# Where an attention + MLP-mixer kernel computes the flag that decides on its general path

## The chip, the cores and the metric

The kernel runs on one core of one Trainium2 chip. The metric is the device time of one execution in microseconds (us), as the median over runs. The engines are TensorE (PE, whose weight loads are shown apart as PEld), VectorE (DVE), ScalarE (ACT), GpSimd (POOL) and SyncE (SP). Each has its own instruction stream and runs it in order; an instruction can wait for semaphores that other engines or landed DMAs count up.

## The reference, cut to what matters

Batch 8, 8 heads, 576 positions, head size 64. For each batch and head the kernel computes causal attention with a bias that comes from a running sum of `s`, and over the result (576 x 512 per batch) an MLP mixer: two products over positions, then two over channels.

```
cum    = cumsum(max(s, 0))
scores = q @ k.T / 8  + min(-(cum[i] - cum[j]), 0)      (j <= i)
x      = softmax(scores) @ v, heads side by side          (576 x 512)
u      = x + (relu(x.T @ w_tok1) @ w_tok2).T
out    = u + relu(u @ w_ch1) @ w_ch2
```

The fast path of the kernel drops far-away blocks of the attention and takes no maximum before the exponential. That is only right for inputs whose bias falls fast enough and whose q and k are small. So the kernel also computes, on the chip, one number that says whether any row breaks these conditions, reads it into a register on every engine, and branches: at zero the kernel ends, above zero a second, slow and general path (`general`) computes everything again. With these inputs the number is zero, and the branch jumps over the code of the general path.

## The kernel before

A small planner in the kernel (`Plan`) takes a list of operations with their dependencies, the engines that can run them, and an estimated cost, simulates the engines, and emits the instructions in the order of the starting times that come out. On PE the operation with the lowest `prio` among those that can start first is taken; a PE operation's `prio` is a pair whose first number is a rank, some 4 per batch.

For each batch `b` the operations are made in this order: loads, transposes and scores of q and k (`quad`, `pair`), the attention products, the token products (`tok`), and the channel products (`chan`). `chan` has two halves:

- L1106: for each of 12 blocks of 128 hidden channels, four matmuls write a tile `pmx` in PSUM, and ACT or DVE (L1113, L1115) evacuate it with a relu into `gb` (odd batches) or `ga`. The last batch is odd and has 320 columns twice, so 24 such tiles.
- L1131: for each of the five chunks of 128 positions, 12 matmuls write a `pmx` tile, DVE adds `u` (L1139) into a tile `of`, and SP stores it (L1144, L1147). In the last batch the fifth chunk is done in two halves of 256 columns.

There are four `pmx` tiles (128 x 512, one PSUM bank each), taken in turn.

The flag is made of four steps at the end of the list. DVE writes the tile `bad` (64 x 4 gaps and 128 x 32 sums of squares against their bounds, L1210). PE sums `bad` over the partitions with a matmul against a column of ones (L1214), into one row of 36 values of a `pmx` tile. DVE sums that row (L1219) and casts it to an integer (L1220), `flagi`. Behind the planned part, `nc.values_load(flagi)` (L1255) makes every engine load the value into a register (TENSOR_LOAD), and `tc.If` (L1258) makes every engine compare and branch. The code behind the branch (rows of L1258 and L1285 in the profile) sets semaphores to what they would be behind the general path, and SP waits there for every semaphore of the kernel before all engines meet and the program ends.

The matmul of the flag has `prio=(100, 0)`: its rank is above that of all others (the last batch's channel products have ranks up to 42), so PE does it last. The two DVE steps have `prio=50`.

Of the kernel before, what the change touches and what calls it, by code (L numbers as in the profile page):

```python
# [246 lines left out]
def c_pe(n, f32=False):  # L247
    occ = n * (4 if f32 else 1) / 2400.0 + 0.0025
    return occ, occ + 0.21
# [131 lines left out]
def kernel(  # L381
# [14 lines left out]
    B, H, S, D = q.shape  # L396
# [21 lines left out]
    def sb(name, shape, dt, pool=None):  # L418
        return (pool or const).tile(shape, dt, name=name, tag=name)
# [44 lines left out]
    P = Plan()  # L464
# [52 lines left out]
    for i in range(2, 4):  # L517
        P.op({"DVE": (0.3, 0.5, lambda i=i: pads(nc.vector, i)), "POOL": (0.4, 0.6, lambda i=i: pads(nc.gpsimd, i))},
             writes=[("pad", i)], prio=40)
    P.op({"DVE": (0.6, 0.8, lambda: pads2(nc.vector)), "POOL": (1.0, 1.2, lambda: pads2(nc.gpsimd))},  # L520
         writes=["padw"], prio=41)
    P.op({"DVE": (0.3, 0.5, lambda: pads3(nc.vector, 1)), "POOL": (0.5, 0.7, lambda: pads3(nc.gpsimd, 1))},
         writes=["padv"], prio=42)
# [12 lines left out]
    def dve(n, fn, two=False):  # L536
        return {"DVE": (*c_dve(n, two), fn)}
# [7 lines left out]
    for ti, src in enumerate((k, q)):  # L545
# [4 lines left out]
        for f in range(2):  # L550
            def cast0(eng, ti=ti, f=f):
# [4 lines left out]
                else:  # L556
# [3 lines left out]
                 reads=[("stage", ti)], writes=[(first, ti, f)], prio=-6)  # L560
    P.op({"SP": (0.6, 4.8, lambda: nc.sync.dma_start(out=s_sb[:, :], in_=s.rearrange("b h s -> (b h) s")))},
         writes=["s"], prio=-7)
    P.op(dve(576, lambda: nc.vector.tensor_scalar_max(out=s_sb[:, :], in0=s_sb[:, :], scalar1=0.0)),
         reads=["s"], writes=["sr"], prio=-1)
    scan = P.op({"DVE": (1.3, 1.6, lambda: nc.vector.tensor_tensor_scan(
        out=cum[:, :], data0=one_sb[:, :], data1=s_sb[:, :], initial=0.0, op0=ALU.mult, op1=ALU.add))},
        reads=["sr"], writes=["cum"], prio=2)
    P.op(dve(1, lambda: nc.vector.tensor_scalar(
        out=half[:, :], in0=cum[:, S - 1 : S], scalar1=-0.5, scalar2=None, op0=ALU.mult)),
        reads=["cum"], writes=["half"], prio=-1)  # L570
    P.op(act(576, lambda: nc.scalar.activation(
        out=wn[:, 0:S], in_=cum[:, :], func=AF.Exp, bias=half[:, 0:1], scale=1.0), True),
        reads=["half", "cum"], writes=["wn"], prio=-5)
    P.op({"ACT": (1.0, 1.1, lambda: nc.scalar.copy(out=neg[:, :, :],
                                                   in_=zero[:, :].unsqueeze(1).to_broadcast([128, 2, 512])))},
         writes=["neg0"], prio=-6)
# [33 lines left out]
    bad = sb("bad", [128, 4 + NSQ], FP32, fast)  # L610
# [346 lines left out]
    def either(n, fa, fd, two=False):  # L957
        return {"ACT": (*c_act(n), fa), "DVE": (*c_dve(n, two), fd)}
# [131 lines left out]
    def chan(b, u, us, uT):  # L1090
        P.shift = SHIFT["chan"][b]
        odd = b % 2
        rank = 4 * (b + 1) + LAG
        g = Buf(r_gb if odd else r_ga)
        spans = [(0, 256), (256, 640)] if b == 1 else [(0, 320), (320, 640)] if odd else [(0, 256), (256, 512)] if b == 0 else [(0, 512)]
        for (cc, (a, e)) in ([(cc, sp) for hf in range(2) for sp in spans for cc in range(6 * hf, 6 * hf + 6)] if b < 2 else
                             [(cc, sp) for cc in range(NCC) for sp in spans]):
            if True:
                ukeys = ([(uT, c, m) for c in range(2) for m in range(NMC)] if b < 1 and a == 0 else
                         [(uT, c) for c in range(a // 128, (e + 127) // 128)])  # L1100
                pm = Buf(r_mx, False)
                n = e - a

                def mm(cc=cc, pm=pm, a=a, e=e):
                    for m in range(NMC):
                        nc.tensor.matmul(out=pm.t[:, 0 : e - a], lhsT=wc1[:, m, cc * 128 : cc * 128 + 128],  # L1106
                                         rhs=uT.t[:, m, a:e], start=(m == 0), stop=(m == NMC - 1))
                P.op({"PE": (4 * c_pe(n)[0], 4 * c_pe(n)[0] + 0.21, mm)},
                     reads=ukeys + [("wc1", cc // (NCC // 2) * 2 + m) for m in range(2)],
                     writes=[(pm, 0)],  # L1110
                     holds=[g], prio=(rank + (cc // 6 + 0.05 * (cc % 6) + 0.4 * (a > 0) if b < 2 else 2.0 * cc / NCC), 0)).late = 2.0
                P.op(either(n,
                            lambda cc=cc, pm=pm, a=a, e=e: nc.scalar.activation(  # L1113
                                out=g.t[:, cc, a:e], in_=pm.t[:, 0 : e - a], func=AF.Relu),
                            lambda cc=cc, pm=pm, a=a, e=e: nc.vector.tensor_scalar_max(  # L1115
                                out=g.t[:, cc, a:e], in0=pm.t[:, 0 : e - a], scalar1=0.0)),
                     reads=[(pm, 0)], writes=[(g, cc, a)], prio=0)
        for ci, c in enumerate((4, 0, 1, 2, 3) if odd else (0, 1, 2, 3)):
            if odd:
                src, si = (us, 0) if c == NJ - 1 else (u, c)  # L1120
            else:
                src, si = u, c
            sk = [(us, 0, 0), (us, 0, 64)] if src is us else [(u, si, 0)]
            o = Buf(r_o, False)
            whole = b < B - 1 or ci < NJ - 1
            for (na, ne) in ([(0, DM)] if whole else [(0, DM // 2), (DM // 2, DM)]):
                pm = Buf(r_mx, False)
                for th in range(3):
                    def mm(c=c, pm=pm, th=th, na=na, ne=ne):
                        for cc in range(th * 4, th * 4 + 4):  # L1130
                            nc.tensor.matmul(out=pm.t[:, na:ne], lhsT=g.t[:, cc, c * 128 : c * 128 + 128],  # L1131
                                             rhs=wc2[:, cc, na:ne], start=(cc == 0), stop=(cc == NCC - 1))
                    occ = 4 * c_pe(ne - na)[0]
                    P.op({"PE": (occ, occ + 0.21, mm)},
                         reads=[(g, cc, a) for cc in range(th * 4, th * 4 + 4) for (a, e) in spans] + [("wc2", i) for i in range(th * 4 // 3, (th * 4 + 3) // 3 + 1)],
                         writes=[(pm, 0)], holds=[o], prio=(rank + 2.0 + 2.0 * ci / NJ, 1 + (na > 0)))

                def add(pm=pm, o=o, src=src, si=si, na=na, ne=ne):
                    nc.vector.tensor_tensor(out=o.t[:, na:ne], in0=pm.t[:, na:ne], in1=src.t[:, si, na:ne], op=ALU.add)  # L1139
                P.op(dve(ne - na, add), reads=[(pm, 0)] + sk, writes=[(o, na)], prio=0)  # L1140

                def st(o=o, c=c, na=na, ne=ne):
                    if c < NJ - 1:
                        nc.sync.dma_start(out=out[b, c * 128 : c * 128 + 128, na:ne], in_=o.t[:, na:ne])  # L1144
                    else:
                        for i in range(2):
                            nc.sync.dma_start(out=out[b - 1 + i, NQ:S, :], in_=o.t[i * 64 : i * 64 + 64, :])  # L1147
                P.op({"SP": (0.6 if c < NJ - 1 else 1.2, 0, st)}, reads=[(o, na)], prio=0, dma=128 * 0.088 / 16)
# [36 lines left out]
    for b in range(B):  # L1185
        for h in range(0, H, 4):
            quad(b, h)
        st = tok(b)
        chan(b, *st)
        P.shift = 0.0  # L1190
        if b == 2:
            behind(b, st[2])
            stage_in(5)
            stage_in(6)
        if b == 3:
            behind(b, st[2])
            stage_in(7)
        if b == B - 3:
            behind(b, st[2])
            for i in range(2):  # L1200
                for h in range(0, H, 4):
                    stage_sq(i, h)
# [3 lines left out]
        reads=["wn", "late"], writes=["pre"], prio=50)  # L1206
# [5 lines left out]
        reads=[("sq", i) for i in range(NSQ)] + ["bad0"], writes=["bad"], prio=50)  # L1212
    bf = Buf(r_mx, False)
    P.op({"PE": (0.3, 0.6, lambda: nc.tensor.matmul(out=bf.t[0:1, 0 : 4 + NSQ], lhsT=ones[:, :], rhs=bad[:, :],  # L1214
                                                    start=True, stop=True))},
         reads=["bad"], writes=[(bf, 0)], prio=(100, 0))

    def flag():
        nc.vector.tensor_reduce(out=flagf[:, :], in_=bf.t[0:1, 0 : 4 + NSQ], op=ALU.add, axis=mybir.AxisListType.X)  # L1219
        nc.vector.tensor_copy(out=flagi[:, :], in_=flagf[:, :])  # L1220
    P.op({"DVE": (0.4, 0.7, flag)}, reads=[(bf, 0)], writes=["flag"], prio=50)

    order = P.run()
    rest = [1.2]
# [65 lines left out]
```

## Time and profile before

| what | us |
|---|---|
| median of 3 runs | 297.11 (296.98 to 297.3) |
| the profiled execution, its own time | 297.6 |
| its span, first to last instruction | 295.8 |
| PE busy | 284.9 |
| granted TensorE clock, mean | 0.997 |

The profiled execution took 297.6 us, of which 295.8 us are its span; 1.8 us lie around it. The profile's own views are: the page (busy time of each engine, groups of instructions), the chain of waits (followed back from the last piece of engine work), the instructions of one line, the waits of one engine, the timeline, and the DMA queues. Times in a row are microseconds from the span's start unless they are marked ns. A `q` behind an engine's name (DVEq, SPq) marks what its sequencer does by itself: waits, register loads, branches, DMA issues.

### The profile page before, as it was taken

To read this page: it belongs to the slowest core of one execution; us is meant where nothing else is said; L and a number is where in the kernel's file an instruction comes from. 1 tells how busy PE (TensorE), PEld (TensorE's weight loads), DVE (VectorE), ACT (ScalarE), POOL (GpSimd) and SP (SyncE) were. 2 spreads that over 40 slices of the span, in tenths; PEclk is the share of its full clock that TensorE was granted. 3 is DMA by queue.
4 is the path that set the end of the run, shared out by engine and by line. 5 is a ranking of instruction groups with operands and counts; after the bars stand their busy time and mean duration, and the time that the engine had idled before them with its cause. 6 is when DMAs were issued, how large, how long until landed. Compare 5 with 4: busy or idle time off the path is not lost.

```text
span 295.8 us, 7107 instructions
## 1 busy us (share of the span) xinstructions
PE 284.9 (96%) x2852; PEld 167.8 (57%) x2885; DVE 196.3 (66%) x425; ACT 195.3 (66%) x311; POOL 82.8 (28%) x147
## 2 busy tenths in 40 slices
PE   8999999999999999999999999999999999999991
PEld 3468665676745555546754555457765544457550
DVE  5894669999999969997577658767679524110030
ACT  5786877889999488996865467047999344227300
POOL 8645669688001954019000000017000000000000
PEclk9999999999999999999999999999999999999998
DMA  7999999999906899759915200259904311320032
GB/s 222 225 207 208 204 211 234 200 248 204 193 9 137 167 261 236 120 133 170 219 25 123 74 35 2 57 142 160 196 4 74 107 71 38 89 106 2 7 106 75
DMA packets 38344, 39.22 MB, mean 133 GB/s; under 512 B 17600, under 2 KB 30976, under 8 KB 38304
## 3 DMA queue, kind: packets, MB, share of 16 engines
q0 software_dynamic: 17072, 24.25, 44.7%
q1 hardware_dynamic: 21232, 14.44, 17.8%
q8 instruction: 24, 0.39, 0.5%
q14 instruction: 16, 0.13, 0.2%
HBM read 40.65 MB, written 9.44 MB: 169 GB/s over the span
## 4 chain that ended last, share of the span: by engine, by line
PE 74%; DMA 14%; DVE 4%; POOL 3%; issue 2%; POOLq 0%; DVEq 0%
PE pmx L1131 28%; PE pmx L1106 28%; DMA vf<-in_v_dram 8%; DMA wc<-in_moe_w_ch_dram 6%; PE pmx L987 4%; PE pmx L1049 4%; PE psc L886 4%; PE psc L803 4%; PE pmx L746 2%; POOL vf L644 1%; DVE ub L1056 1%; POOL qkn L491 1%; DVE vp L662 1%; DVE x L919 1%; DVE h L1001 0%
## 5 line engine op out<-in xcount | busy, mean ns | idle before, releaser
L823 ACT ACTIVATE E<-psc 128x1024 bf16<-128x1024 f32 x64 | 62.1, 1022 | 27.1 <-PE psc L803 27.0
L1106 PEld LDWEIGHTS <-wc 128*128 128x128 bf16 x624 | 58.9, 98 | 32.1 <-issue 0.5
L1106 PE MATMUL pmx<-uTb,wc 128*128 128x320 bf16 (+2 forms) x384 | 55.7, 299 | 0.5 <-DVE gb L1115 0.5
L1131 PE MATMUL pmx<-wc,gb 128*128 128x512 bf16 (+1 forms) x243 | 54.0, 369 | 0.7 <-issue 0.3
L1106 PE MATMUL pmx<-uTa,wc 128*128 128x512 bf16 (+1 forms) x234 | 45.3, 336 | 0.3
L1113 ACT ACTIVATE gb<-pmx 128x320 bf16<-128x320 f32 (+2 forms) x65 | 28.3, 438 | 24.7 <-PE pmx L1106 20.0
L1131 PE MATMUL pmx<-wc,ga 128*128 128x512 bf16 x186 | 43.6, 379 | 0.5 <-issue 0.2
L1131 PEld LDWEIGHTS <-gb 128*128 128x128 bf16 x252 | 23.9, 98 | 24.5
L678 ACT ACTIVATE junk<-qkn 128x1152 bf16<-128x1152 bf16 x32 | 37.3, 1166 | 0.5
L1113 ACT ACTIVATE ga<-pmx 128x512 bf16<-128x512 f32 (+1 forms) x45 | 24.1, 545 | 19.2 <-PE pmx L1106 18.5
L644 POOL DMA_DIRECT2D vf<-in_v_dram x39 | 33.4, 870 | 3.8 <-DMA vf<-in_v_dram 1.9
L1131 PEld LDWEIGHTS <-ga 128*128 128x128 bf16 x192 | 17.9, 98 | 20.1
L662 DVE TENSOR_TENSOR vp<-vf,wT 128x512 bf16<-128x512 f32 (+1 forms) x39 | 26.0, 712 | 1.1 <-DMA vf<-in_v_dram 0.8
L886 PEld LDWEIGHTS <-E 128*128 128x128 bf16 x576 | 21.2, 97 | 5.0
L919 DVE TENSOR_TENSOR x<-psc,rc 128x640 bf16<-128x640 f32 x28 | 23.0, 820 | 0.7
L832 DVE TENSOR_TENSOR E<-E,keep 128x512 bf16<-128x512 bf16 x56 | 22.4, 414 | 1.3 <-ACT E L823 1.2
L471 POOL CAST seen<-uTb 1x1 f32<-1x1 bf16 x10 | 2.0, 198 | 74.6 <-DMA uTb<-ub 70.5
L1139 DVE TENSOR_TENSOR of<-pmx,ua 128x512 f32<-128x512 f32 x16 | 11.3, 707 | 15.5 <-PE pmx L1131 9.7
L769 DVE COPY kT<-pmx 128x576 bf16<-128x576 bf16 x20 | 14.6, 751 | 9.6 <-PE pmx L746 9.5
L803 PEld LDWEIGHTS <-kT 64*128 64x128 bf16 x320 | 12.9, 94 | 13.8 <-issue 11.8
L886 PE MATMUL psc<-vp,E 128*128 128x65 bf16 x522 | 20.5, 193 | 0.0
L769 DVE COPY qT<-pmx 128x576 bf16<-128x576 bf16 x21 | 15.2, 752 | 8.0 <-PE pmx L746 7.3
(119 smaller groups left out, 336.7 us busy)
## 6 DMA issues: line engine op xcount, KB each, us to landing
vf<-in_v_dram POOLq DMA_DIRECT2D x32, 256.0 KB, 7.8
out_dram<-of SPq DMA_DIRECT2D x31, 256.0 KB, 2.1
qkn<-in_k_dram POOLq DMA_DIRECT2D x19, 288.0 KB, 7.2
qkn<-in_q_dram POOLq DMA_DIRECT2D x19, 288.0 KB, 7.8
wc<-in_moe_w_ch_dram POOLq DMA_DIRECT2D x8, 384.0 KB, 8.5
out_dram<-of SPq DMA_DIRECT2D x10, 128.0 KB, 2.3
vf<-in_v_dram POOLq DMA_DIRECT2D x7, 128.0 KB, 8.3
gb<-in_k_dram SPq DMA_DIRECT2D x1, 576.0 KB, 3.8
```

What stands on the lines that cost most here:

```text
L644: nc.gpsimd.dma_start(out=vf.t[p0 : p0 + n, c, :, :], in_=v[b, :, c * 128 : c * 128 + n, :].rearrange("h p d -> p h d"))
L662: eng.tensor_tensor(out=vp.t[p0 : p0 + n, c, :, 0:D], in0=vf.t[p0 : p0 + n, c, :, :], in1=wT[p0 : p0 + n, cw, b * H : b * H + H].unsqueeze ...
L678: nc.scalar.activation(out=junk[:, :].rearrange("p (t n) -> p t n", t=2), in_=i, func=AF.Square, accum_out=sq[:, col : col + 1])
L769: nc.vector.tensor_copy(out=o, in_=i)
L803: nc.tensor.matmul(out=ps.t[:, hh * 512 + c0 : hh * 512 + c0 + e - a], lhsT=kT.t[hh * 64 : hh * 64 + 64, j0 : j0 + 128], rhs=qT.t[hh * 64 ...
L823: nc.scalar.activation(out=E.t[:, :, 512 * pc : 512 * pc + 512], in_=ps.t[:, :].rearrange("p (e n) -> p e n", e=2), func=AF.Exp, scale=0.125)
L832: nc.vector.tensor_tensor(out=o, in0=o, in1=keep[:, :].unsqueeze(1).unsqueeze(1).to_broadcast([128, 2, 2, 128]), op=ALU.mult)
L886: nc.tensor.matmul(out=o[:, ic, 0:DE], lhsT=E.t[:, hh, d0 : d0 + 128], rhs=vp.t[:, jc, h + 2 * hh, 0:DE], start=(jc == j_lo), stop=(jc == ic))
L919: nc.vector.tensor_tensor(out=x.t[:, :, :].rearrange("p c (g f e d) -> p g e f c d", f=2, e=2, d=D)[:, h // 4, h % 2], in0=pav2()[:, :, :, ...
L1106: nc.tensor.matmul(out=pm.t[:, 0 : e - a], lhsT=wc1[:, m, cc * 128 : cc * 128 + 128], rhs=uT.t[:, m, a:e], start=(m == 0), stop=(m == NMC ...
L1113: lambda cc=cc, pm=pm, a=a, e=e: nc.scalar.activation(out=g.t[:, cc, a:e], in_=pm.t[:, 0 : e - a], func=AF.Relu),
L1131: nc.tensor.matmul(out=pm.t[:, na:ne], lhsT=g.t[:, cc, c * 128 : c * 128 + 128], rhs=wc2[:, cc, na:ne], start=(cc == 0), stop=(cc == NCC - 1))
```

## The change

`chan` of the last batch notes the PE operation that makes the last of the 24 tiles of L1106 under the name "last". The flag's matmul now also depends on it and has rank 0 instead of 100: the planner puts it as soon as this product is done, ahead of the products of L1131. The two DVE steps have `prio` 0 instead of 50. Nothing else is edited, and what is computed is the same. Line numbers behind the two new lines are higher by 2: the flag's matmul is L1216, the DVE steps are L1221 and L1222, the adds L1141, the stores L1146 and L1149, the register loads L1257, the branch L1260.

```diff
@@ chan, behind the loop over the 24 tiles
+        if b == B - 1:
+            P.writer["last"] = P.ops[-2]
         for ci, c in enumerate((4, 0, 1, 2, 3) if odd else (0, 1, 2, 3)):
...
     P.op({"PE": (0.3, 0.6, lambda: nc.tensor.matmul(out=bf.t[0:1, 0 : 4 + NSQ], lhsT=ones[:, :], rhs=bad[:, :],
                                                     start=True, stop=True))},
-         reads=["bad"], writes=[(bf, 0)], prio=(100, 0))
+         reads=["bad", "last"], writes=[(bf, 0)], prio=(0, 0))
...
-    P.op({"DVE": (0.4, 0.7, flag)}, reads=[(bf, 0)], writes=["flag"], prio=50)
+    P.op({"DVE": (0.4, 0.7, flag)}, reads=[(bf, 0)], writes=["flag"], prio=0)
```

What the build makes of it, at three places. In the rows, `of_112` to `of_115` are the four output tiles, `pmx_118` to `pmx_121` the four PSUM tiles, `gb_111` the evacuated hidden channels, `wc_70` and `wc_71` the channel weights, and the names in brackets are the counters that an instruction waits for (DVE_49, PE_49, Activation_49 of the engines, DMAHW of landed stores).

DVE at the end of the program, before:

```order
L1139 TENSOR_TENSOR of_115<-pmx_121,us_107 128x512 [waits DVE_49,DMAHW5_49,PE_49,Activation_49]
L1139 TENSOR_TENSOR of_112<-pmx_120,ub_105 128x512 [waits DVE_49,DMAHW6_49,PE_49,Activation_49]
L1139 TENSOR_TENSOR of_113<-pmx_118,ub_105 128x512 [waits DVE_49,DMAHW7_49,PE_49,Activation_49]
L1139 TENSOR_TENSOR of_114<-pmx_119,ub_105 128x512 [waits DVE_49,DMAHW0_49,PE_49,Activation_49]
L1139 TENSOR_TENSOR of_115<-pmx_121,ub_105 128x256 [waits DMAHW1_49,DMAHW2_49,DVE_49,PE_49]
L1139 TENSOR_TENSOR of_115<-pmx_120,ub_105 128x256 [waits PE_49]
L1219 TENSOR_REDUCE flagf<-pmx_118 1x1 [waits PE_49]
L1220 CAST flagi<-flagf 1x1 [waits DVE_49]
L1255 TENSOR_LOAD flagi [waits DVE_49]
L1258 COMPARE_AND_BRANCH
```

DVE at the same place now:

```order
L1221 TENSOR_REDUCE flagf<-pmx_121 1x1 [waits PE_49]
L1222 CAST flagi<-flagf 1x1 [waits DVE_49]
L1141 TENSOR_TENSOR of_115<-pmx_120,us_107 128x512 [waits DMAHW5_49,PE_49,Activation_49]
L1141 TENSOR_TENSOR of_112<-pmx_118,ub_105 128x512 [waits DMAHW6_49,PE_49,Activation_49]
L1141 TENSOR_TENSOR of_113<-pmx_119,ub_105 128x512 [waits DMAHW7_49,PE_49,Activation_49]
L1141 TENSOR_TENSOR of_114<-pmx_121,ub_105 128x512 [waits DMAHW0_49,PE_49]
L1141 TENSOR_TENSOR of_115<-pmx_120,ub_105 128x256 [waits DMAHW1_49,DMAHW2_49,DVE_49,PE_49]
L1141 TENSOR_TENSOR of_115<-pmx_118,ub_105 128x256 [waits PE_49]
L1257 TENSOR_LOAD flagi [waits DVE_49]
L1260 COMPARE_AND_BRANCH
```

The two steps of the flag stand ahead of the last batch's six adds, and the register load follows directly on the last add. Four of the adds have one wait less, each of them an instruction of its own: DVE's code ahead of the branch is four instructions shorter.

SP ahead of the branch, before:

```order
L1144 DMA out_dram<-of_114 128x512 [waits DMAHW0_49,DVE_49]
L1147 DMA out_dram<-of_115 64x512 [waits DMAHW1_49,DVE_49]
L1147 DMA out_dram<-of_115 64x512 [waits DMAHW2_49]
L1144 DMA out_dram<-of_112 128x512 [waits DMAHW3_49,DVE_49]
L1144 DMA out_dram<-of_113 128x512 [waits DMAHW4_49,DVE_49]
L1144 DMA out_dram<-of_114 128x512 [waits DMAHW5_49,DVE_49]
L1144 DMA out_dram<-of_115 128x256 [waits DMAHW6_49,DVE_49]
L1144 DMA out_dram<-of_115 128x256 [waits DMAHW7_49,DVE_49]
L1255 TENSOR_LOAD flagi [waits DVE_49]
L1255 ISA x2
L1258 COMPARE_AND_BRANCH
```

SP at the same place now:

```order
L1146 DMA out_dram<-of_114 128x512 [waits DMAHW0_49,DVE_49]
L1257 TENSOR_LOAD flagi [waits DVE_49]
L1257 ISA x2
L1149 DMA out_dram<-of_115 64x512 [waits DMAHW1_49,DVE_49]
L1149 DMA out_dram<-of_115 64x512 [waits DMAHW2_49]
L1146 DMA out_dram<-of_112 128x512 [waits DMAHW3_49,DVE_49]
L1146 DMA out_dram<-of_113 128x512 [waits DMAHW4_49,DVE_49]
L1146 DMA out_dram<-of_114 128x512 [waits DMAHW5_49,DVE_49]
L1146 DMA out_dram<-of_115 128x256 [waits DMAHW6_49,DVE_49]
L1146 DMA out_dram<-of_115 128x256 [waits DMAHW7_49,DVE_49]
L1260 COMPARE_AND_BRANCH
```

SP's load of the flag, and its wait for it, have moved ahead of the last batch's seven stores; its branch stays behind them.

PE between the last tile of L1106 and the first chunk of L1133 (L1131 before) now:

```order
L1106 LDWEIGHTS wc_70
L1106 MATMUL pmx_119<-uTb_109,wc_70 128x320
L1216 MATMUL pmx_121<-bad,ones 1x36 [waits Activation_49]
L1133 LDWEIGHTS gb_111
L1133 MATMUL pmx_120<-wc_71,gb_111 128x512 [waits Activation_49]
```

Before, the matmul of the flag was PE's last one, behind the last product of the two half chunks. Now the flag takes the `pmx` tile that the first chunk had, and the chunks move on by one tile. On ACT and POOL nothing moves: their load of the flag follows their last work (evacuations, loads of q and k) as before, and on PE it follows its last product.

## The prediction

> **What bounds the kernel now.** I read the page first, then the chain of waits from 270 us on, then the lines of the register load and the branch, since the change can only act there.
>
> ```profile
> span 295.8 us, 7107 instructions
> ...
> PE 284.9 (96%) x2852; PEld 167.8 (57%) x2885; DVE 196.3 (66%) x425; ACT 195.3 (66%) x311; POOL 82.8 (28%) x147
> ```
>
> PE is busy for 96% of the span, and the change takes no product from it. What is left is the tail. The chain's last rows (start, us, what):
>
> ```profile
> 289.30 0.42 DVE of L1139
> 289.72 0.10 DVE flagf L1219
> 289.82 0.02 issue
> 289.85 0.14 DVE flagi L1220
> ```
>
> The last add runs from 289.30 to 289.72, the flag's two steps end at 289.85 + 0.14 = 289.99, and engine work is over. The span goes on for another 5.8 us. The lines of the load and the branch show what is in them (each row: count, then ns of one as min/median/max, then first and last start):
>
> ```profile
> L1255 ACTq TENSOR_LOAD <-flagi x1: 467/467/467, 290.0 to 290.0; - x1
> L1255 POOLq TENSOR_LOAD <-flagi x1: 492/492/492, 290.0 to 290.0; - x1
> L1255 DVEq TENSOR_LOAD <-flagi x1: 546/546/546, 290.0 to 290.0; - x1
> L1255 PEldq TENSOR_LOAD <-flagi x1: 492/492/492, 290.0 to 290.0; - x1
> L1255 SPq TENSOR_LOAD <-flagi x1: 538/538/538, 290.1 to 290.1; - x1
> ```
>
> ```profile
> L1258 SPq EVENT_SEMAPHORE  x8: 17/17/17, 291.6 to 292.1; - x8
> L1258 ACTq COMPARE_BRANCH  x1: 50/50/50, 290.5 to 290.5; - x1
> L1258 POOLq COMPARE_BRANCH  x1: 45/45/45, 290.6 to 290.6; - x1
> L1258 PEldq COMPARE_BRANCH  x1: 3773/3773/3773, 290.6 to 290.6; - x1
> L1258 DVEq COMPARE_BRANCH  x1: 72/72/72, 290.6 to 290.6; - x1
> L1258 SPq COMPARE_BRANCH  x1: 58/58/58, 291.1 to 291.1; - x1
> L1258 POOLq EVENT_SEMAPHORE  x1: 17/17/17, 291.1 to 291.1; - x1
> L1258 ACTq EVENT_SEMAPHORE  x1: 17/17/17, 293.6 to 293.6; - x1
> L1258 PEldq EVENT_SEMAPHORE  x1: 51/51/51, 294.5 to 294.5; - x1
> L1258 DVEq EVENT_SEMAPHORE  x1: 21/21/21, 294.7 to 294.7; - x1
> ```
>
> All five engines wait for the flag, load it in about 0.5 us and branch. COMPARE_BRANCH is the jump, and EVENT_SEMAPHORE the first instruction behind it: POOL and SP are back after 0.5 us, ACT after 3.1, PE after 3.9, DVE only after 4.1. SP then waits for all others (waits of SP, then its rows of the closing line):
>
> ```profile
> SPq L1285 <- DVEq L1258: 2.0, 1, 2.0
> ```
>
> ```profile
> L1285 SPq EVENT_SEMAPHORE  x14: 17/28/2038, 292.2 to 295.8; - x14
> ```
>
> SP's longest wait, 2.0 us, is ended by DVE's first instruction behind the jump at 294.7; 1.1 us later the span ends. So the chain that sets the end is: last add, flag, DVE's load at 290.0, DVE's jump (back at 294.7), closing steps to 295.8. From the start of DVE's load to the end: 5.8 us.
>
> What fills the jump are fetches of code: in 290 to 296 us (a DMA view; one slice of the GB/s row is 0.15 us)
>
> ```profile
> GB/s 0 0 0 41 280 341 205 7 0 0 164 0 55 55 55 0 0 0 0 0 0 0 0 0 0 0 0 0 55 0 0 0 0 0 109 55 0 0 0 0
> ...
> q8 instruction: 2, 0.03, 2.4%
> q14 instruction: 6, 0.05, 2.4%
> ```
>
> the bytes up to 291.2 are the last store, those from 291.5 (slice 10) on are instructions, 0.9 us behind the branches at 290.6. [...]
>
> **The change part by part.** *The flag's inputs.* They are ready long before:
>
> ```profile
> L1210 DVE TENSOR_SCALAR bad<-sq x1: 170/170/170, 230.9 to 230.9; 128x32 f32<-128x32 f32 x1
> ```
>
> ```profile
> L1113 ACT ACTIVATE gb<-pmx x24: 437/437/437, 263.8 to 276.3; 128x320 bf16<-128x320 f32 x24
> ```
>
> `bad` is there at 231 us. The `pmx` tile that the flag takes is the oldest of the last four, evacuated four steps before ACT's last one at 276.3, so PE does not wait for it. The flag is then due at about 277, while DVE idles: its reduce and cast (0.17 + 0.14 us) cost nothing there.
>
> *SP's load.* It now waits for the flag ahead of the seven stores. SP's next store (timeline):
>
> ```profile
> 278.97 0.69 DVE L1139 TENSOR_TENSOR of<-pmx,us 128x512 f32<-128x512 f32 x1 [15.00 <-PE pmx L1131]
> 279.68 1.12 SPq L1147 DMA_DIRECT2D out_dram<-of  x2
> ```
>
> is at 279.68; a load from 277 to 278 is over by then. Nothing, with some 1.7 us to spare.
>
> *ACT and POOL* jump at about 278 and are back long before the end: off the path.
>
> *PE.* The matmul of the flag leaves the end and enters the stream of products. Its rows at the old place (timeline):
>
> ```profile
> 289.19 0.09 PEld L1214 LDWEIGHTS pmx<-bad,ones 128*1 128x1 f32 x2 [0.21 <-issue]
> 289.19 0.23 PE L1214 MATMUL pmx<-bad,ones 128*1 128x36 f32 x2
> ```
>
> Two passes of 194 ns end 0.23 us after the first began, so the second starts 0.04 us behind the first: at least 2 x 0.04 = 0.08 us. At most it is idle time and both passes, 0.21 + 0.23 = 0.44. The idle time holds the streaming of the product ahead of it, which a stream of products has anyway, so I take 0.2, nearer the lower end. All of L1131, the last add and the last store come 0.2 us later: last add at 289.50.
>
> *DVE's load* no longer waits for the flag, but stands right behind the last add. Does it start while that add still runs, or behind it? No row shows a load there. The nearest one is DVE's wait instructions behind adds:
>
> ```profile
> 263.28 0.69 DVE L1139 TENSOR_TENSOR of<-pmx,ua 128x512 f32<-128x512 f32 x1 [1.90 <-DMA out_dram<-of]
> ...
> L1139 DVEq EVENT_SEMAPHORE  x3: 21/2436/15559, 263.4 to 279.1; - x3
> ```
>
> The first starts at 263.4 while its add runs until 263.97, the last at 279.1 beside the add of 278.97: the sequencer goes on within 0.1 us. I take the same for the load: 289.50 + 0.05 = 289.55. The other bound is the add's end, 289.50 + 0.42 = 289.92.
>
> *The sum.* DVE's load starts at 289.55 instead of 290.0; everything behind it, 5.8 us, is taken as it is, DVE's 4.1 us stall included, since its own row is the nearest. End at 295.35 instead of 295.8: 0.45 us less. What would be late next: PE's load can start at 289.0 + 0.2 = 289.2 and it is back 4.5 us later, at 293.7, DVE at 289.55 + 4.7 = 294.25. SP branches behind the last store:
>
> ```profile
> L1144 SPq DMA_DIRECT2D out_dram<-of x1: 332/332/332, 289.8 to 289.8; - x1
> ```
>
> at 289.8 + 0.2 + 0.33 = 290.3, and came to its wait for DVE 1.6 us behind its branch (291.1 to 292.7), so at about 292.0. DVE stays last. The profiled execution would take 297.6 - 0.45 = 297.15; it lies 0.5 above the median of the runs, so on the median 297.11 - 0.45 = 296.66.
>
> A measurement of this kernel can tell about 0.2%, 0.6 us, from no change. The forecast lies just inside it. With the flag's matmul at its bounds (0.08 to 0.44) it is 296.5 to 296.9.
>
> **The rivals.** *The stalls shrink.* Before, three far jumps fetch at once, ACT's first (3.1 us), then PE's (3.9) and DVE's (4.1). Now ACT's is 11 us earlier and PE's 0.3 or more ahead of DVE's. If waiting for each other made the last ones long, DVE needs 3.1 us: back at 289.55 + 0.6 + 3.1 = 293.25, and PE's return at 293.7 and the closing 1.1 us end the span at 294.8, 1.0 less: 296.1; with PE at 3.1 too, DVE is last again and the end is 294.35: 295.65. The order of the three speaks for it; that packets are done well before any return (the last of the first bunch at 292.25, DVE back at 294.7) speaks against. A second way to this end: DVE's code is four instructions shorter, so its target may now lie in code that is resident, as POOL's and SP's do; then PE's 293.7 is last: 296.1. [...]
>
> *DVE's load is held until the last add has ended.* Then it starts at 289.92 + 0.05 = 289.97, and 0.05 us are left: 297.05. The wait instructions above speak against it, but they touch no data, and a load reads memory. [...]
>
> *Slower: DVE's fetch meets the last store.* Before, the store's bytes were through at 291.2 and instructions came from 291.5. Now the store is 0.2 later and the fetch, 0.9 us behind a branch at 290.15, is due at 291.05, inside it. The store lands
>
> ```profile
> DMA to landing us min/median/max: 1.7/1.7/1.7
> ```
>
> 1.7 us after its issue at 290.0, at 291.7. If the fetch is only served then, DVE is back 0.65 later than in the sum: 0.2 slower than before, 297.3. It decides once the fetch waits longer than 0.45 us. Against it: the store's bytes use few of the slices, and only 128 KB are left.
>
> **How the numbers follow.** Forecast as summed 0.40, shrinking stalls 0.34, held load 0.16, the store in the way 0.07, something not seen 0.03. The likeliest gives 296.65. The range goes from the lower rival's end, 295.6, to 297.2, beyond the held load; left out is the slower case and what was not seen. Faster by over 0.2% (below 296.5): the shrinking stalls and the lower edge of the forecast, 0.40. Slower by over 0.2% (above 297.7) needs more than the store's 0.2 us: 0.04. Within: 0.56.
>
> **What would show it.** Right: the flag's cast at about 277, SP's load over before 279.9, ACT and POOL back before 283; the last add at 289.5; DVE's load starting within 0.1 us of it, and DVE back 4.7 us later, still the last one that SP waits for; span 295.3. The shrinking stalls show as DVE back in under 3.6 us after its branch, the held load as a load behind 289.9, the store as instruction packets later than 1.2 us behind DVE's branch. The prediction is wrong if the stream of products is stretched by more than 0.44 us, or if SP waits last for another engine than DVE or PE.

## The result, and the profile after

| | us |
|---|---|
| before, median of 6 runs | 297.11 (296.71 to 297.3) |
| after, median of 6 runs | 294.91 (294.62 to 295.22) |
| ratio | 0.9928, 95% interval 0.9915 to 0.9941 |
| profiled execution after, its own time | 294.74 |
| its span | 292.9 |

The kernel is 2.2 us faster (1.8 to 2.5 by the interval). The forecast was 0.45. The two spans differ by more, 2.9 us, because the part ahead of the tail also lies at another place in each execution: a second profile of the kernel before, below, has its last add 1.0 us later than the first with the same code. So the tail is compared from the start of the last add.

First the end of the chain of waits after (start, us, what):

```profile
269.90 5.57 PE pmx L1106 x41
275.47 0.15 PE pmx L1216 x2
275.63 13.10 PE pmx L1133 x72
...
288.75 0.42 DVE of L1141
```

The flag's matmul (L1216) is a link of PE's stream now, and the last engine work is the last add. From its start at 288.75 to the end of the span it is 4.1 us; before it was 295.8 - 289.30 = 6.5. The tail is 2.4 us shorter. The timeline around the flag shows what was paid for that:

```profile
274.63 0.84 PE L1106 MATMUL pmx<-uTb,wc 128*128 128x320 bf16 x5
...
275.40 0.23 PE L1216 MATMUL pmx<-bad,ones 128*1 128x36 f32 x2
...
275.56 4.92 PE L1133 MATMUL pmx<-wc,gb 128*128 128x512 bf16 x22
275.67 0.18 DVE L1221 TENSOR_REDUCE flagf<-pmx 1x1 f32<-1x36 f32 x1 [12.50 <-PE pmx L1216]
275.88 0.14 DVE L1222 CAST flagi<-flagf 1x1 int32<-1x1 f32 x1
...
279.14 1.13 SPq L1149 DMA_DIRECT2D out_dram<-of  x2
```

The products of L1106 follow each other by 0.136 us (5.57 / 41 in the chain), so behind the five from 274.63 on the next one could have started at 274.63 + 5 x 0.136 = 275.31. It starts at 275.56: the flag costs the stream 0.25 us. That and the shorter tail make -2.4 + 0.25 = -2.15 us, about the 2.2 between the medians.

The register loads and the branch (count, ns of one as min/median/max, first and last start):

```profile
L1257 SPq TENSOR_LOAD <-flagi x1: 479/479/479, 276.1 to 276.1; - x1
...
L1257 PEldq TENSOR_LOAD <-flagi x1: 487/487/487, 286.6 to 286.6; - x1
L1257 DVEq TENSOR_LOAD <-flagi x1: 546/546/546, 288.8 to 288.8; - x1
```

```profile
L1260 SPq EVENT_SEMAPHORE  x8: 17/17/17, 290.1 to 291.2; - x8
L1260 ACTq COMPARE_BRANCH  x1: 50/50/50, 276.6 to 276.6; - x1
...
L1260 POOLq EVENT_SEMAPHORE  x1: 17/17/17, 277.1 to 277.1; - x1
L1260 ACTq EVENT_SEMAPHORE  x1: 17/17/17, 279.3 to 279.3; - x1
L1260 PEldq COMPARE_BRANCH  x1: 3877/3877/3877, 287.2 to 287.2; - x1
L1260 DVEq COMPARE_BRANCH  x1: 72/72/72, 289.4 to 289.4; - x1
...
L1260 DVEq EVENT_SEMAPHORE  x1: 21/21/21, 290.0 to 290.0; - x1
L1260 PEldq EVENT_SEMAPHORE  x1: 51/51/51, 291.1 to 291.1; - x1
```

The reader is to see three things. ACT and POOL are done at 279. DVE loads beside its last add, at 288.8, as forecast, but it is back 0.6 us behind its branch, not 4.1. And PE loads at 286.6 and jumps at 287.2, while its products run on until 288.7; its 3.9 us jump is over at 291.1, where the forecast had 293.7.

So who is last? SP's longest waits from 288 us on, its closing rows, the last store's landing, and the queues of code in 288 to 294 us:

```profile
SPq L1260 <- SPq L1260: 1.1, 3, 0.5
SPq L1287 <- PEq L1287: 0.7, 2, 0.5
```

```profile
L1287 SPq EVENT_SEMAPHORE  x14: 17/28/28, 291.2 to 292.8; - x14
```

```profile
DMA to landing us min/median/max: 1.9/1.9/1.9
```

```profile
q8 instruction: 2, 0.03, 2.2%
q14 instruction: 3, 0.02, 1.4%
```

No wait of SP names an engine's jump any more (PEq L1287 is the meeting of the engines), and none of its closing waits is longer than 0.028 us, where one took 2.038 before. What SP is held by now is the landing of the last store: issued at 289.2 and 1.9 us under way, it is down at 291.1; the eighth of SP's rows on L1260, its wait for this store, follows at 291.2, and the closing waits and the meeting take the last 1.7 us. PE is back at 291.1 too, but SP's closing waits come to PE's counter only at 291.8, 0.7 us later. Three packets of code come on q14 in these six us, where there were six: two at 290.6 and 290.7, and one at 293.5, behind the end of the span. None lies between DVE's branch (289.4) and its return (290.0). The bound has passed from a jump to the stores.

### The profile page after: what moved, and what is told of

Read it like the earlier page. It is cut to its first block, busy times and chain, and to the rows that moved or that the text cites. A ratio compares the mean times of both kernels' runs of the same rounds, so it can differ in the third digit from the quotient of the medians.

```text
span 292.9 us, 7136 instructions
## 1 busy us (share of the span) xinstructions
PE 286.8 (98%) x2885; PEld 167.5 (57%) x2885; DVE 196.5 (67%) x425; ACT 195.0 (67%) x311; POOL 82.8 (28%) x147
## 4 chain that ended last, share of the span: by engine, by line
PE 76%; DMA 13%; DVE 5%; POOL 3%; issue 1%; POOLq 0%; DVEq 0%
PE pmx L1133 29%; PE pmx L1106 28%; DMA vf<-in_v_dram 7%; DMA wc<-in_moe_w_ch_dram 6%; PE pmx L987 5%; PE pmx L1049 4%; PE psc L886 4%; PE psc L803 4%; PE pmx L746 2%; DVE vp L662 1%; POOL qkn L491 1%; DVE x L919 1%; DVE ub L1056 1%; POOL seen L471 1%; POOL vf L644 1%
## 5 line engine op out<-in xcount | busy, mean ns | idle before, releaser
L1106 PEld LDWEIGHTS <-wc 128*128 128x128 bf16 x624 | 58.9, 98 | 31.8 <-issue 0.2
L1106 PE MATMUL pmx<-uTb,wc 128*128 128x320 bf16 (+2 forms) x384 | 55.7, 300 | 0.2 <-DVE gb L1115 0.2
L1133 PE MATMUL pmx<-wc,gb 128*128 128x512 bf16 (+1 forms) x252 | 55.0, 369 | 0.0
L1106 PE MATMUL pmx<-uTa,wc 128*128 128x512 bf16 (+1 forms) x240 | 45.6, 337 | 0.0
L1133 PE MATMUL pmx<-wc,ga 128*128 128x512 bf16 x192 | 44.5, 380 | 0.0
L1133 PEld LDWEIGHTS <-gb 128*128 128x128 bf16 x252 | 23.7, 98 | 24.5
L1133 PEld LDWEIGHTS <-ga 128*128 128x128 bf16 x192 | 17.9, 98 | 20.1
L1141 DVE TENSOR_TENSOR of<-pmx,ua 128x512 f32<-128x512 f32 x16 | 11.3, 709 | 15.0 <-PE pmx L1133 9.3
L803 PE MATMUL psc<-qT,kT 64*128 64x256 bf16 (+2 forms) x320 | 20.3, 250 | 0.0
```

What stands on the lines that cost most here:

```text
L803: nc.tensor.matmul(out=ps.t[:, hh * 512 + c0 : hh * 512 + c0 + e - a], lhsT=kT.t[hh * 64 : hh * 64 + 64, j0 : j0 + 128], rhs=qT.t[hh * 64 ...
```

## The experiments

Two reasons why DVE's 4.1 us are gone were to be told apart: its code ahead of the branch is four instructions shorter, so that its target may have come near; and three far jumps no longer start at once. The rival was that the flag's place alone explains the gain. Below, a jump is called near where the engine is back in 0.6 us or less, and far where it needs 2.4 us or more; "resident" is the author's word for code at which an engine is back before any packet of code has come, as POOL before (back at 291.1, first packet at 291.5). Where the code lies is in no profile. Each ratio is to the kernel before, timed on the same chip.

**DVE's target moved back.** Four steps that are never executed are put into the general path on DVE:

```diff
+            gz = gp.tile([128, 8], FP32, name="gz", tag="gz")
+            for i in range(4):
+                nc.vector.memset(gz[:, i : i + 1], 0.0)
```

> The changed kernel with four small DVE memsets added inside the general path, which is not executed: no instruction that runs is different, but the code that DVE jumps over is four instructions longer, so its target stands where it stood before the change. Theory A (the target had come into code that was resident): DVE's return from the jump takes 4.1 us again instead of 0.6, DVE is last again, back at about 293.5 in the changed kernel's times, and the time is 294.91 + 1.7 = 296.6, close to the recorded forecast; if a fetch without ACT's beside it takes 3.1 us, 295.6. Theory B (DVE's return was short because no other engine was fetching): nothing changes, 294.9.

Measured: 295.92 us (10 runs), ratio 0.9961 (0.9946 to 0.9975). Branch rows and SP's wait (lines are 3 higher):

```profile
L1263 DVEq COMPARE_BRANCH  x1: 72/72/72, 289.6 to 289.6; - x1
...
L1263 PEldq EVENT_SEMAPHORE  x1: 51/51/51, 291.3 to 291.3; - x1
L1263 DVEq EVENT_SEMAPHORE  x1: 21/21/21, 292.6 to 292.6; - x1
```

```profile
SPq L1290 <- DVEq L1263: 0.7, 1, 0.7
```

The far jump is back, and with it the wait of SP for DVE, but at 3.0 us and not at 4.1; the page counts one packet of code more on q14 than that of the changed kernel (16, not 15). This version keeps 1.15 us of the gain, and 1.0 us goes with four instructions that are never run. The two intervals (0.9915 to 0.9941, 0.9946 to 0.9975) only just do not meet; together with the rows of the branch they show that the place of the target matters. The kernel was profiled once more:

> The kernel with four more instructions in the general path on DVE once more, beside the two others: DVE's far jump alone takes 2.9 to 3.2 us (2.97 and 3.16 in the two profiles with such a jump), 295.1 to 296.8 us. If it takes 3.6 us or more, the size of one such jump varies from execution to execution and no difference below 1 us between single profiles can be put down to the other engines' jumps.

Measured: 3.0 us again, in one run of 296.19 us; both lie where they were expected.

**Where the edge lies.** The same with two steps (`range(2)`):

> As the first run, with two memsets instead of four: where the edge of the resident code lies. Theory A: either as the changed kernel (DVE back in 0.6 us, 294.9) or as with four (4 us, 296.6), by the side of the edge on which the target falls; if the edge falls between DVE's first instruction behind the jump and its next, the first comes after 0.6 us and the next some 4 us later, 296.3. Theory B: 294.9.

Measured: 294.91 us in one run.

```profile
L1263 DVEq COMPARE_BRANCH  x1: 72/72/72, 289.6 to 289.6; - x1
...
L1263 DVEq EVENT_SEMAPHORE  x1: 21/21/21, 290.2 to 290.2; - x1
```

With two instructions more the jump is still near (0.6 us), with four it is far. The kernel before had four more. The change came to the near side by two or three instructions, which nobody placed there: that part of the gain is luck.

**The flag much earlier.** The flag's matmul no longer waits for the last tile of L1106:

```diff
-         reads=["bad", "last"], writes=[(bf, 0)], prio=(0, 0))
+         reads=["bad"], writes=[(bf, 0)], prio=(0, 0))
```

> The changed kernel, but the flag's matmul depends only on its inputs, so the flag is made at about 231 us, long before the last batch's channel products. DVE's code ahead of the branch has by chance as many instructions as in the kernel before, four more than in the changed one. Theory A (DVE's target must be in resident code): the early flag alone brings only the 0.4 to 0.5 us of the forecast, 296.6 to 296.7, with DVE back some 4 us behind its branch. Theory B (an early flag separates the jumps, and that makes them short): 294.9, like the changed kernel.

Measured: 295.35 us (8 runs), ratio 0.9944 (0.9926 to 0.9963).

```profile
L1260 DVEq COMPARE_BRANCH  x1: 72/72/72, 289.2 to 289.2; - x1
...
L1260 DVEq EVENT_SEMAPHORE  x1: 21/21/21, 292.4 to 292.4; - x1
```

In this order DVE has the wait instructions of the kernel before again, as many ahead of the branch and as many behind it, and its jump is far: 3.2 us. So the same code of DVE returns after 4.1 us in the kernel before and after 3.2 here; the difference is not in the place of DVE's target. Neither expectation holds whole: the jump is far, as the first said, but it takes less than 4 us, and 295.35 us lies between the two. That an earlier flag is no better is all that the time shows; the interval overlaps that of the changed kernel.

**The kernel before with DVE's target near.** In the general path the memsets and casts of the loads go from DVE to POOL, which makes the code that DVE jumps over 14 instructions shorter:

```diff
-                nc.vector.memset(f[64:128, NJ - 1, :, :], 0.0)
+                nc.gpsimd.memset(f[64:128, NJ - 1, :, :], 0.0)
...
-                nc.vector.tensor_copy(out=t[:, :, :, :], in_=f[:, :, :, :])
+                nc.gpsimd.tensor_copy(out=t[:, :, :, :], in_=f[:, :, :, :])
```

> The kernel before, its flag late, but with the casts and memsets of the general path (not executed) moved from DVE to POOL: DVE jumps over 14 instructions less. Theory A: DVE is back 0.6 us behind its branch, at about 291.2 instead of 294.7, although ACT and PE fetch at the same time; PE, back at 294.5, is then last, and the time falls only by some 0.25 us, to 296.85. Theory B: DVE is back 4.1 us behind its branch, 297.1.

Measured: 297.2 us (12 runs), ratio 1.0014 (0.9999 to 1.0029).

```profile
L1258 ACTq COMPARE_BRANCH  x1: 50/50/50, 290.2 to 290.2; - x1
...
L1258 DVEq EVENT_SEMAPHORE  x1: 21/21/21, 290.9 to 290.9; - x1
L1258 PEldq EVENT_SEMAPHORE  x1: 51/51/51, 293.8 to 293.8; - x1
L1258 ACTq EVENT_SEMAPHORE  x1: 17/17/17, 293.9 to 293.9; - x1
```

DVE's jump is near with the flag at its late place too, so it is the target that decides and not the time. The time does not fall, not even by the 0.25 us that were expected (the interval ends at 0.9999): ACT and PE are last instead, ACT now after 3.6 us. A near target on DVE alone brings nothing that can be measured while two other far jumps stand at the end. One thing stays open here: in this profile and in its repeat the tail is 0.4 to 0.7 us shorter than before, and the timed runs show none of it.

> The kernel before with the shorter code of the general path on DVE, profiled once more: only ACT and PE jump far, at the same time. If far jumps wait for each other, two at once lie between one and three: the later of the two returns 3.3 to 3.8 us behind its branch (3.63 before), and the time is 296.5 to 298. If not, 2.6 to 3.0 us on ACT, as in the kernels where ACT jumps 11 us earlier.

The repeat (one run, 297.13 us) has 3.8 us for both ACT and PE, at the upper end of what was expected.

**Three far jumps at once, repeated.** The kernel before, profiled again:

> The kernel before, unchanged, profiled once more, to see how far the length of its far jumps repeats. If far jumps wait for each other, the three at once again make DVE's the longest, at 3.8 us or more, and the last return is DVE's; the time is 296.5 to 297.9. If the 4.1 us were a chance of one execution, DVE's lies at 3.0 to 3.4 us like the single far jumps (2.97, 3.04, 3.16, and ACT's 3.27).

Measured: 298.63 us in one run, 0.7 above the range that was named.

```profile
L1258 ACTq COMPARE_BRANCH  x1: 50/50/50, 291.5 to 291.5; - x1
...
L1258 DVEq COMPARE_BRANCH  x1: 72/72/72, 291.6 to 291.6; - x1
...
L1258 PEldq EVENT_SEMAPHORE  x1: 51/51/51, 295.0 to 295.0; - x1
L1258 ACTq EVENT_SEMAPHORE  x1: 17/17/17, 295.6 to 295.6; - x1
L1258 DVEq EVENT_SEMAPHORE  x1: 21/21/21, 295.8 to 295.8; - x1
```

DVE's stall is 4.1 us again and the last; ACT's is 4.1 this time instead of 3.1, PE's 3.4 instead of 3.8. ACT's stall differs by a microsecond between the two executions and PE's by 0.4; DVE's, the last of the three, does not.

**One and two far jumps at the end.** To the changed kernel, once with and once without the four unexecuted steps on DVE, a step on ACT is added that copies one number of the last `pmx` tile, which nothing uses, so that ACT's load and jump come at the end:

```diff
+                if b == B - 1 and na > 0:
+                    P.op({"ACT": (0.2, 0.3, lambda pm=pm, na=na: nc.scalar.activation(
+                        out=lateact[:, :], in_=pm.t[0:1, na : na + 1], func=AF.Relu))},
+                        reads=[(pm, 0)], writes=["lateact"], prio=0)
```

> The kernel with four more instructions in the general path on DVE (DVE's jump is far again, 3.0 us), and with one added step on ACT behind the last product (it copies one number, which nothing uses), so that ACT's load and far jump come at the end too, beside DVE's. Theory 'together': far jumps take longer when their fetches meet; then DVE's jump takes 3.6 to 4.2 us instead of 3.0, ACT's 2.9 to 3.4 instead of 2.6, and the time is 0.5 to 1.2 us above the kernel with DVE's far jump alone: 296.4 to 297.1. Rival 'own size': 3.0 against 4.1 us came from where the target lies and not from the others; then DVE stays within 2.9 to 3.2 us and the time within 0.2 us of 295.9.

> The changed kernel with the same added step on ACT, so that ACT's far jump alone comes at the end, while DVE's stays near. ACT takes 0.2 us for the step, 0.5 for its load and then 2.5 to 2.8 us for its jump, so it is back at about 292.2 us on the changed kernel's scale, where SP's closing waits begin to end. Theory 'one late far jump costs what it exceeds the stores by': 295.1 to 295.5, 0.2 to 0.6 above the changed kernel. Rival 'any late far jump costs the whole of what was gained': 296.5 or above.

Measured with both far: 295.76 us (4 runs), ratio 0.9949 (0.9931 to 0.9966). With ACT's alone: 295.81 us (10 runs), ratio 0.9959 (0.9947 to 0.9971). The branch rows, of the first and of the second:

```profile
L1268 DVEq COMPARE_BRANCH  x1: 72/72/72, 290.1 to 290.1; - x1
...
L1268 ACTq COMPARE_BRANCH  x1: 50/50/50, 290.5 to 290.5; - x1
...
L1268 DVEq EVENT_SEMAPHORE  x1: 21/21/21, 293.4 to 293.4; - x1
L1268 ACTq EVENT_SEMAPHORE  x1: 17/17/17, 293.6 to 293.6; - x1
```

```profile
L1265 ACTq COMPARE_BRANCH  x1: 50/50/50, 290.9 to 290.9; - x1
...
L1265 ACTq EVENT_SEMAPHORE  x1: 17/17/17, 294.1 to 294.1; - x1
```

and the end of the second one's chain of waits:

```profile
289.88 0.44 DVE of L1142
...
290.34 0.16 ACT lateact L1145
```

Neither expectation of the first kernel holds whole: DVE's stall is 3.3 us beside ACT's, which is less than the 3.6 asked for by the theory and more than the 3.2 of its rival, a difference of 0.2 us in one profile; the time is the rival's, since it is not above that of DVE's far jump alone. In the second, one far jump on ACT costs 0.9 us against the changed kernel (0.9959 against 0.9928), more than the 0.2 to 0.6 expected and less than the rival's 1.6: the added step came behind the last add's end (290.34), 0.45 us later than I had reckoned, and ACT's jump took 3.3 us here, where it takes 2.75 in the changed kernel, far from the end.

**No far jump at all.** The general path is cut to one DMA in both kernels (they leave out the general path, so they are no replacement for it):

```diff
         nc.sync.dma_start(out=scr[:, :], in_=cum[:, :])
-        with tc.For_i(0, B, 1) as b:
...
```

> The kernel before, with the general path cut to a single DMA, so that every engine's jump is short (it leaves out the general path, which these inputs do not take). Theory 'stalls': what the late flag costs is mostly that three far jumps (ACT 3.1, PE 3.8, DVE 4.1 us) begin at the very end; without code to jump over, all five are back in about 0.6 us and only the closing steps of SP (some 1.5 us) follow the flag. Expected 295.1 us, 2.0 less than before, and the longest jump at most 0.7 us. Rival 'place': the flag's late place costs by itself, by its matmul, reduce and cast and five loads behind the last product, whatever the jumps cost; then no more than 0.5 us goes and the time is 296.6 or above.

> The changed kernel, with the same cut (it leaves out the general path). Theory 'stores are last': in the changed kernel DVE's jump costs 0.6 us already, and the end is set by the last store's landing (a late slice, which PE's fetch of code may have delayed by some 0.3 us) and SP's closing waits; without PE's fetch the end comes 0 to 0.4 us earlier: 294.5 to 294.9, against 294.9. Its difference to the kernel before with the same cut is what the flag's place is worth where jumps are cheap: 0.3 to 0.6 us. Rival 'PE's jump is last': PE's far jump (3.9 us, back at 291.1) sets the end in the changed kernel; then the cut takes 0.8 us or more: 294.1 or below.

Measured on one chip: before with the cut 295.32 us (4 runs), ratio 0.993 (0.991 to 0.995); after with the cut 294.72 (4 runs), ratio 0.9921 (0.9891 to 0.9951). What 'stalls' and 'stores are last' expected holds. The rival 'place' falls. The rival 'PE's jump is last' is not excluded by four runs, whose interval reaches down to 293.9 us (0.9891); what speaks against it is the changed kernel's profile, where SP is not held by PE. Where nothing is far, the late flag costs no more than can be measured (0.3 us between the two ratios, 0.6 between the medians, and the intervals overlap). And within that interval, 0.9 us either way, the change has what there is to get: without any code to jump over, the changed kernel is not measurably faster. Of the second kernel it has to be said that in its build DVE's last add and SP's last store stand behind the branch, so that its tail (3.5 us in the table below) is not the changed kernel's with the jumps taken out.

The cut kernel with the late flag ends by something else than expected, a cost that had been hidden. Closing rows of POOL:

```profile
L1184 POOLq EVENT_SEMAPHORE  x4: 17/17/17, 293.3 to 294.0; - x4
L1184 POOLq DRAIN  x3: 51/107/2510, 290.7 to 293.8; - x3
```

POOL's first DRAIN behind the branch takes 2.5 us, 290.7 to 293.3, and all engines meet only then. In the kernel before it lay under the jumps (291.1 to 293.7); in the changed kernel it is over at 279.7. In the changed kernel with the cut, the last store lands as fast as before, and the page counts 22 packets on q8, where the changed kernel's has 24:

```profile
DMA to landing us min/median/max: 1.7/1.7/1.7
```

**A safer margin.** The changed kernel with the general path's steps moved from DVE to POOL as above:

> The changed kernel, with the memsets and casts of the general path's loads moved from DVE to POOL, so that DVE jumps over 14 instructions less and its target stands farther inside the code that is resident. Theory 'edge': DVE's jump is near in the changed kernel already (0.58 us), so nothing changes: 294.9, and DVE back within 0.7 us. Rival 'chance of the placement': the short jump comes from something else, such as the state of the fetch queue; then the time may move to 295.4 to 295.9 as in the two kernels where DVE's jump took 3 us.

Measured: 295.17 us (4 runs), ratio 0.9922 (0.99 to 0.9945), with DVE back after 0.6 us. It is the changed kernel's ratio; the time itself is higher, as is that of the kernel before on this chip (297.44). Nothing is gained, but DVE's target stands some 14 instructions farther from the edge.

All together; the stalls are from branch to return in us, those of jumps at the end in bold:

| kernel | ratio | last add to end | ACT | PE | DVE |
|---|---|---|---|---|---|
| before (two profiles) | 1 | 6.5, 6.6 | **3.1, 4.1** | **3.8, 3.4** | **4.1, 4.1** |
| before, DVE near (two) | 1.0014 | 5.9, 6.2 | **3.6, 3.8** | **3.5, 3.8** | 0.6, 0.6 |
| before, cut | 0.993 | 4.8 | 0.2 | 0.3 | 0.2 |
| DVE and ACT far at the end | 0.9949 | 5.1 | **3.1** | 4.0 | **3.3** |
| ACT far at the end | 0.9959 | 5.2 | **3.3** | 3.8 | 0.6 |
| four more on DVE (two) | 0.9961 | 4.7, 4.8 | 2.6, 2.7 | 3.9, 4.0 | **3.0, 3.0** |
| flag at 231 us | 0.9944 | 4.9 | 2.7 | 4.2 | **3.2** |
| after | 0.9928 | 4.1 | 2.8 | 3.9 | 0.6 |
| two more on DVE | one run | 4.1 | 2.6 | 3.9 | 0.6 |
| after, general path's steps on POOL | 0.9922 | 4.1 | 2.4 | 3.9 | 0.6 |
| after, cut | 0.9921 | 3.5 | 0.2 | 0.3 | 0.4 |

The tails are from one or two profiles each. With the 0.25 us of the stream taken off where the flag is early, they agree with the ratios within some 0.4 us, except for 'before, DVE near', where the tail says 0.4 to 0.7 us less and the runs 0.4 us more.

The packets of code on q14 separate near from far as well. In the profiles of before and after, a near jump of DVE, POOL or SP goes with one packet and a far jump of ACT or DVE with two, of which the second starts 0.6 us behind the return: six packets from the first branch to the end of the span before, five in the changed kernel. The pages of all twelve profiles that have the general path agree: 16 packets on q14 where ACT and DVE jump far, 15 where ACT alone does.

## Why the prediction was wrong, step by step

The sign of the forecast was right, its size was a fifth of what came, and 294.91 lies below the range.

**What held.** The flag is cast at 275.9 and SP's load is over two microseconds ahead of its next store. ACT and POOL are back long before the end. The stream pays 0.25 us for the matmul (0.2 forecast). DVE's load starts at 288.8 while the add of 288.75 runs until 289.17, so the held load did not come. The flag's own place is therefore worth what the sum said: the load stands 0.01 us behind the last add's start instead of 0.73 (289.30 to 290.03), less 0.25 in the stream, makes 0.47 us.

**What failed: "everything behind it, 5.8 us, is taken as it is, DVE's 4.1 us stall included, since its own row is the nearest".** From DVE's load to the end it is 4.1 us now. The row was right for its place and wrong for the new one, on two grounds, both of which the prediction had named as ways of the rival "the stalls shrink" and held for less likely than no change. That the stall keeps its length at the new place was the author's estimate from that one row, and no run shows it: DVE is back after 0.6 us in the changed kernel, and after 3.0 to 3.2 us where its target is far and it branches behind the others.

- *DVE's stall shrinks when the three far jumps no longer start together.* In the two kernels where DVE's target is far and only DVE branches behind the last add, the stall is 3.0 to 3.2 us (three profiles) instead of 4.1 (two), and in one of them (the flag at 231 us) DVE's code is as long as in the kernel before. PE's far jump, begun 2 us earlier, is still under way there. In steps, for ACT and DVE: one far jump at the end 3.0 to 3.3, both together 3.1 and 3.3, ACT beside PE's 3.6 and 3.8, all three 3.1 to 4.1. That far jumps lengthen each other is what this order points to, and it is not shown. PE's stall does not follow it: 3.8 to 4.2 us where PE jumps ahead of the others, 3.4 to 3.8 where it jumps with them. Nor is ACT's 3.3 us alone at the end against 2.4 to 2.75 earlier explained by other jumps. How it comes about was not isolated; the packets of code do not fill the time, since in the profile of the kernel before DVE is back at 294.7, 2.6 us behind the start of the last q14 packet of the bunch that follows the branches (292.1), and in the first with four more instructions on DVE it is back at 292.6, some 1.6 us behind it (about 291.0, by a DMA view with slices of 0.175 us); such a packet takes 0.3 to 0.5 us. Worth: 1.0 us of the tail.
- *The target is near.* Four instructions less on DVE take the stall from 3.0 to 0.6 us. With two instructions back in it is still near (0.6 us), with four it is far. Since the last store is next, only 4.7 - 4.1 = 0.6 us of the 2.4 shows in the tail; by the timed runs it is 1.0 (0.9961 against 0.9928).

The sum of the parts: 0.47 + 1.0 + 0.6 = 2.1 us, against 2.2 measured. How it splits between the last two is known to some 0.4 us only: the version with four more instructions on DVE keeps 1.15 us by the timed runs, where 0.47 + 1.0 would be 1.5.

**What failed beside it: PE's load at 289.2 and its return at 293.7.** This number kept even the rival's forecast too high, at 296.1. It took PE's load to follow on PE's last product as it stood in the trace of before. There the load had to wait for the flag, the last thing computed. Without that wait PE's sequencer takes the load and the jump 2 us ahead of its array (286.6, last products until 288.7), so most of the 3.9 us lies under products and the last add. The bound then falls to the stores, which the sum had SP pass without a wait.

**The rival on the other side** had a fetch meet the last store. One does: a packet of 16 KB on q8 comes from 288.6 to 289.7, while PE alone is in a far jump, beside the last two stores, and the last store takes 1.9 us to land instead of 1.7. Those 0.2 us are on the path now. The store ahead of it, issued at 287.9, loses more, 3.0 us instead of 1.7, and lands only 0.26 us ahead of the last one:

```profile
DMA to landing us min/median/max: 3.0/3.0/3.0
```

Before, both took 1.7 us. In all eight profiles in which PE's far jump starts ahead of the last store, the shortest landing of this line's stores is 1.8 to 2.0 us, and 1.7 in the six others. It was the store that lost and not PE, whose jump took 3.9 us here and 3.8 before, and the price was far below the gain.

**The chances.** 0.40 for a sum that kept every stall was too much, and the reason is in the prediction itself: it counted three simultaneous stalls of rising length, and code of DVE shorter by four instructions, and then used the trace's stall for a situation in which both had changed. That DVE's target would fall on the near side could not be read from the trace of before, and that it did is luck; that the three jumps would come apart could.

## What to carry to other kernels

In this kernel the branch at the end cost what its last engine needed to return, 4.1 us on DVE. That hung on whether the target was near (0.6 us), and it was 1 us longer where three engines jumped at the same time (4.1 us against 3.0 to 3.2). So read a flag out early on every engine that is done, and look at the rows of the branch by engine before pricing it. A duration that was measured while three things happened together need not be what the same thing takes apart. The stall that vanished here by two or three instructions of code length came back, with 3.0 us, by four added elsewhere: give such a one a margin, or shorten what is jumped over.

## What the runs showed of the hardware that was not expected

- A taken branch over the general path costs 0.5 to 0.6 us where the target is near, and 2.4 to 4.2 us where it is far (ACT, PE and DVE, over all profiles); for DVE the edge lies between two and four added instructions. With the path cut to one DMA a branch costs ACT, PE and DVE 0.2 to 0.4 us.
- In the profiles of before and after, a near jump goes with one packet of code on q14 (8 KB), a far jump of ACT or DVE with two: six packets before (two far, two near), five after (one far, three near).
- In the changed kernel PE's sequencer performs a register load and a branch 2 us ahead of the end of the matmuls that stand in front of them (286.6 and 288.7); DVE's load starts beside the add in front of it (288.76 and 288.75).
- With a packet of code of 16 KB on q8 under way beside the last two stores of 128 KB in the changed kernel, they took 3.0 and 1.9 us to land; in the kernel before, 1.7 each.
- POOL's first DRAIN behind the branch takes 2.5 us in all 14 profiles, whether it starts at 233 or at 292 us.
- The same kernel's far jumps differ from execution to execution by up to 1 us on one engine (ACT 3.1 and 4.1), so one profile of a tail is weak evidence for differences below that.
